# FFN of an adaLN transformer block: the last four token tiles as one group of 512 in place of two pairs, with a new order of issue on all engines

## The chip, the core and the metric

The kernel runs on one core of one Trainium2 chip. The metric is the device time of one execution in microseconds (us), lower is better; a time is the median of several executions. A core has a tensor engine (PE, matmuls), a vector engine (DVE), a scalar engine (ACT), a small general engine (POOL) and a sync engine (SP). Each has a queue of its own that it works through in order; an instruction that waits on a semaphore holds all that stand behind it in its queue. Here SP issues every DMA, plain copies and transposing ones alike.

## The reference

One transformer block with adaptive layer norm on x of 2048 tokens by 512 features, all in bfloat16. `c` is a conditioning vector.

```python
mod = (silu(c) @ w_mod).reshape(1, 6, 1, -1)
sa, ca, ga, sb, cb, gb = (mod[:, i] for i in range(6))
h = layernorm(x) * (1 + ca) + sa
x = x + ga * attention(h, wqkv, wo)
h = layernorm(x) * (1 + cb) + sb
x = x + gb * ((silu(h @ w1) * (h @ w3)) @ w2)
```

The attention has 32 heads of 16 features. Each token looks at 8 positions only: itself and those 2, 4, ... 14 tokens before it; positions before the start are masked out of the softmax. The FFN (w1, w3: 512 by 1792, w2: 1792 by 512) does most of the arithmetic.

## The kernel before

**Tiles and stages.** The tokens are 16 tiles of 128. The stages of a tile run through several engines: statistics of the first layer norm on DVE (`ln_stats`, L576; the normalised tile `xn` by L607), a transposition to features by tokens and the scaling with the modulation (`ln_T`, L644), the projections to q, k (`proj_qk`, L710, evicted by ACT L739 and L740) and v (`proj_v`, L744), local attention for pairs of tiles (products of q with shifted k on DVE L781, sums over features on PE L791, softmax with L808, L821, L833, L835, L836 and a transposition of the weights by PE L850; products of v with the weights on DVE L868 and L873, sums on PE L886, evicted to `ac` by ACT L892 and transposed to `ot` by DMA), the output projection (`project`, L895: PE L901, residual on DVE L906, with the sums that the second layer norm needs), the second layer norm (`ln_sums`, L613: ACT L617, L621, L627, POOL L629, ACT L633, L636), its transposition (`ln_T` again), and the FFN. `ffn_unit` (L911) computes one 128-wide piece of the hidden layer of a group of tiles: 4 matmuls with w1, ACT L924 for the silu, 4 matmuls with w3 (all by L918), DVE L933 for the product. There are 14 such units for each group. `ffn_w2` (L940) multiplies with w2 (PE L962; for the last two tiles in halves of 256 columns, L950), and `store` (L970) adds the residual on DVE L972 and sends the tile out.

**v goes through DRAM.** ACT evicts a tile's v from PSUM to one of three buffers, `v0` to `v2` (L760). SP stores it to `v_scratch_dram`, and shifted copies of it are loaded back as `vsh` (L858) for the attention. A buffer can be filled again only when the store of the tile before it has landed.

**wo** comes in four loads of 32 partitions' worth each and is scaled by ga in one DVE instruction (L987), which waits for all four. The output projection L901 waits for that.

**Groups.** `LN1` gives the groups of tiles for the first layer norm and the projections, `FFN` those for the second layer norm and the FFN. A matmul of a unit has as many columns as its group has tokens: 256 for a pair, 512 for four tiles. `DMA_T` says which groups are transposed by DMA (L652, issued by the common line L124, one DMA per tile, followed by four ACT instructions L656 on the whole group) and which by PE (L671, evicted and scaled by L679): the first tuple is for the groups of `LN1`, the second for those of `FFN`.

**The order of the work.** A class `Program` first records every operation with its engine, the values that it reads and writes, and their buffer pools. `ORDER` is a list of the numbers of the operations; `place` (L143) puts each at the end of its engine's queue in that order, and gives the values the buffers in `SLOTS` (eight PSUM banks, three `h`, four `q`, five `xn`, three `v` and others). `synchronize` (L165) works out which semaphores each must wait for, from data and from reuse of buffers, and `emit` (L208) writes the queues. So the two lists decide what stands behind what on every engine.

Of the kernel before, what the change touches and what calls it, by code (L numbers as in the profile page):

```python
# [264 lines left out]
FFN = [[0,1],[2,3],[4,5,6,7],[8,9,10,11],[12,13],[14,15]]  # L265
# [6 lines left out]
DMA_T = ((3, 4), (2, 3, 4, 5))  # L272
# [3 lines left out]
def _build(p, A_x, A_wqkv, A_wo, B_w1, B_w3, B_w2, c, w_mod, out):  # L276
# [364 lines left out]
    def pairs(Ts):  # L641
        return [Ts[i:i + 2] for i in range(0, len(Ts), 2)]

    def ln_T(which, gi, vns):  # L644
        vh = Val("h", hpool)
        vh.pieces = [Val(f"h_{ft}") for ft in range(KT)] if not which and not gi else None
        n = len(vns)
        if gi in DMA_T[which]:
            k = ("tr", 2 * gi + (2 * len(LN1) if which else 0))
# [365 lines left out]
    zold = []  # L1015
    for gi, Ts in enumerate(FFN):
        vns = [v for pr in pairs(Ts) for v in ln_sums(pr)]
# [116 lines left out]
```

## Time and profile before

| | |
|---|---|
| median of 3 runs | 238.24 us (237.93 to 238.61) |
| the profiled execution's own time | 237.94 us |
| its span in the profile | 236.2 us, clock of PE 0.999 of full |
| PE busy | 229.8 us, 97% of the span, 1768 matmul instructions |
| DVE, ACT, POOL busy | 178.8, 147.7 and 20.0 us |
| DMA | 40.42 MB, mean 171 GB/s |

The profile shows one execution. Its span runs from the first to the last recorded instruction; 1.7 us of the execution lie outside it. The page gives the busy time of each engine, the busy share in 40 slices of 5.9 us, and the chain of work that ended last. The timeline gives rows of one engine: start, duration, line, operation, output and input, count, and in brackets the idle time ahead of it and what ended that. SPq is SP's queue: a row there is the time that SP took to issue a DMA, not the time until its data landed; the latter is a line of its own, "DMA to landing". PE can run a weight load beside a matmul. Some matmul records are missing from the trace, so a row's count may be one or two short.

### The profile page before, as it was taken

To read this page: it belongs to the slowest core of one execution; us is meant where nothing else is said; L and a number is where in the kernel's file an instruction comes from. 1 tells how busy PE (TensorE), PEld (TensorE's weight loads), DVE (VectorE), ACT (ScalarE), POOL (GpSimd) and SP (SyncE) were. 2 spreads that over 40 slices of the span, in tenths; PEclk is the share of its full clock that TensorE was granted. 3 is DMA by queue.
4 is the path that set the end of the run, shared out by engine and by line. 5 is a ranking of instruction groups with operands and counts; after the bars stand their busy time and mean duration, and the time that the engine had idled before them with its cause. 6 is when DMAs were issued, how large, how long until landed. Compare 5 with 4: busy or idle time off the path is not lost.

```text
span 236.2 us, 4478 instructions
## 1 busy us (share of the span) xinstructions
PE 229.8 (97%) x1768; PEld 136.0 (58%) x1794; DVE 178.8 (76%) x286; ACT 147.7 (63%) x298; POOL 20.0 (8%) x44
## 2 busy tenths in 40 slices
PE   7999999999999999999999999999999999999995
PEld 5766554544597586564444444444465457485774
DVE  5598999999979999999999999793364403434433
ACT  3299587979989855985746786829866415040300
POOL 5432050002000000110001010001010000000000
PEclk9999999999999999999999999999999999999999
DMA  6999589999999783896591854441311000000202
GB/s 198 391 324 311 140 305 236 220 261 369 359 264 405 280 263 100 255 263 217 147 293 54 305 139 69 86 180 44 76 38 44 25 0 1 0 25 0 71 0 89
DMA packets 42717, 40.42 MB, mean 171 GB/s; under 512 B 23224, under 2 KB 39624, under 8 KB 40648
## 3 DMA queue, kind: packets, MB, share of 16 engines
q1 hardware_dynamic: 42688, 40.14, 57.4%
q8 instruction: 14, 0.23, 0.4%
q14 instruction: 7, 0.06, 0.1%
q10 hardware_dynamic: 8, 0.00, 0.0%
HBM read 30.67 MB, written 4.21 MB: 148 GB/s over the span
## 4 chain that ended last, share of the span: by engine, by line
PE 87%; DMA 4%; ACT 4%; DVE 1%; issue 1%; SPq 1%; POOL 0%; ACTq 0%
PE pall L918 41%; PE pall L962 18%; PE pall L728 7%; PE pall L901 5%; PE pall L750 4%; PE pall L886 3%; PE pall L791 3%; PE pall L950 3%; DMA sb_wm_s<-in_w_mod_dram 2%; DMA v_scratch_dram<-sb_v 2%; PE pall L671 1%; SPq L124 1%; ACT sb_xn L636 1%; ACT sb_xn L621 1%; ACT sb_q L739 1%
## 5 line engine op out<-in xcount | busy, mean ns | idle before, releaser
L918 PE MATMUL pall<-sb_h,sb_w 128*128 128x256 bf16 (+1 forms) x664 | 101.1, 307 | 0.6 <-ACT sb_ac L892 0.2
L918 PEld LDWEIGHTS pall<-sb_h,sb_w 128*128 128x128 bf16 x672 | 65.0, 98 | 35.8 <-issue 1.1
L933 DVE TENSOR_TENSOR sb_hh<-sb_sg,pall 128x256 bf16<-128x256 bf16 (+1 forms) x84 | 39.9, 506 | 36.7 <-PE pall L918 31.2
L924 ACT ACTIVATE sb_sg<-pall 128x256 bf16<-128x256 f32 (+1 forms) x84 | 36.0, 452 | 45.3 <-PE pall L918 41.9
L962 PE MATMUL pall<-sb_w,sb_hh 128*128 128x512 bf16 x190 | 44.0, 379 | 0.3
L781 DVE TENSOR_TENSOR sb_pq<-sb_q,sb_kT 128x4096 bf16<-128x4096 bf16 x16 | 36.4, 2285 | 0.0
L962 PEld LDWEIGHTS pall<-sb_w,sb_hh 128*128 128x128 bf16 x196 | 18.9, 98 | 21.7 <-issue 0.4
L728 PE MATMUL pall<-sb_h,sb_wqkv 128*128 128x512 bf16 (+1 forms) x156 | 30.3, 335 | 0.7 <-issue 0.4
L728 PEld LDWEIGHTS pall<-sb_h,sb_wqkv 128*128 128x128 bf16 x160 | 14.7, 98 | 11.9 <-ACT sb_v L760 0.8
L972 DVE TENSOR_TENSOR sb_o<-pall,sb_x 128x512 bf16<-128x512 f32 (+1 forms) x18 | 11.1, 628 | 9.7 <-PE pall L962 6.0
L629 POOL TENSOR_TENSOR sb_rs<-sb_rs,sb_cst 128x2 f32<-128x2 f32 x8 | 6.8, 855 | 135.4 <-ACT sb_rs L627 135.4
L656 ACT ACTIVATE sb_h<-sb_h,sb_modc 128x512 bf16<-128x512 bf16 (+1 forms) x24 | 16.3, 733 | 3.0 <-DMA sb_h<-sb_xn 3.0
L868 DVE TENSOR_TENSOR sb_vsh<-sb_vsh,sb_al 128x4096 bf16<-128x4096 bf16 x7 | 15.9, 2287 | 0.0
L750 PE MATMUL pall<-sb_wqkv,sb_h 128*128 128x512 bf16 x60 | 15.2, 379 | 0.3 <-issue 0.2
L901 PE MATMUL pall<-sb_wo,sb_ot 128*128 128x512 bf16 x60 | 14.7, 379 | 0.3 <-issue 0.2
L873 DVE TENSOR_TENSOR sb_vsh<-sb_vsh,sb_al 128x2048 bf16<-128x2048 bf16 x12 | 14.3, 1222 | 0.3 <-DMA sb_vsh<-v_scratch_dram 0.2
L892 ACT ACTIVATE sb_ac<-pall 128x512 bf16<-128x512 f32 x16 | 9.6, 604 | 5.7 <-PE pall L886 5.6
L679 ACT ACTIVATE sb_h<-pall,sb_modc 128x256 bf16<-128x256 bf16 (+1 forms) x18 | 9.8, 614 | 4.7 <-DVE sb_modc L536 3.8
L636 ACT ACTIVATE sb_xn<-sb_x,sb_nb,sb_rs 128x512 bf16<-128x512 bf16 x16 | 12.6, 807 | 0.1
L906 DVE SCALAR_TENSOR_TENSOR sb_x<-pall,sb_x 128x512 bf16<-128x512 f32 x16 | 10.9, 687 | 1.6 <-PE pall L901 1.5
L621 ACT ACTIVATE sb_xn<-sb_x,sb_nm 128x512 bf16<-128x512 bf16 x16 | 11.4, 715 | 0.2
L740 ACT ACTIVATE sb_kT<-pall 128x512 bf16<-128x512 f32 x16 | 9.4, 604 | 3.1 <-PE pall L728 3.1
(94 smaller groups left out, 212.7 us busy)
## 6 DMA issues: line engine op xcount, KB each, us to landing
sb_vsh<-v_scratch_dram SPq DMA_DIRECT2D x13, 1024.0 KB, 7.2
sb_w<-in_B_w_dram SPq DMA_DIRECT2D x6, 512.0 KB, 6.6
sb_vshx<-v_scratch_dram SPq DMA_DIRECT2D x3, 1024.0 KB, 6.5
sb_w<-in_B_w_dram SPq DMA_DIRECT2D x6, 384.0 KB, 6.3
sb_x<-in_A_x_dram SPq DMA_DIRECT2D x8, 256.0 KB, 6.9
v_scratch_dram<-sb_v SPq DMA_DIRECT2D x16, 128.0 KB, 6.2
out_dram<-sb_o SPq DMA_DIRECT2D x14, 128.0 KB, 2.3
sb_wqkv<-in_A_wqkv_dram SPq DMA_DIRECT2D x6, 256.0 KB, 6.3
```

Source lines behind the costliest of these rows:

```text
L636: p.op("act", lambda e, vn=vn, T=T: e.activation(vn.at[:], x_sb[:, T, :], ACT.Identity, bias=nb[:, T, :], scale=rs[:, NT + T, :]), c_act(5 ...
L656: return e.activation(vh.at[:, ft, 0:n * P], vh.at[:, ft, 0:n * P], ACT.Identity, bias=modc[:, 8 * which + ft:8 * which + ft + 1], scale=m ...
L728: ins = e.matmul(bank(vp)[:, j * n:(j + 1) * n], wqkv[:, t, col:col + P], vh.at[:, t, 0:n], start=(t == ORDER[0] and j == 0), stop=(t == O ...
L750: ins = e.matmul(bank(vp), vh.at[:, t, tt * P:(tt + 1) * P], wqkv[:, t, 2 * D:3 * D], start=(t == ORDER[0]), stop=(t == ORDER[-1]))
L781: return e.tensor_tensor(vp.at[:], in0, in1, ALU.mult)
L868: return e.tensor_tensor(v_w, v_w, a_w, ALU.mult)
L873: return e.tensor_tensor(v_w, v_w, a_w, ALU.mult)
L901: ins = e.matmul(bank(vy), bass.AP(vt.at, ft * 2 * P + a, [[KT * 2 * P, P], [step_, P]]), wo[:, ft, :], start=(ft == 0), stop=(ft == KT - 1))
L918: ins = e.matmul(bank(vp)[:, 0:n], wt[:, t, fi * P:(fi + 1) * P], vh.at[:, t, 0:n], start=(t == 0), stop=(t == KT - 1))
L924: p.op("act", lambda e: e.activation(vt.at[:, 0:n], bank(vgp)[:, 0:n], ACT.Silu), c_act(n), k, r=[vgp], w=[vt], table="silu")
L933: p.op("dve", lambda e: e.tensor_tensor(vh_.at[:, 0:n], vt.at[:, 0:n], bank(vup)[:, 0:n], ALU.mult), c_dve(n), k, r=[vt, vup], w=[vh_])
L962: ins = e.matmul(bank(vz), vhh[fi].at[:, tt * P:(tt + 1) * P], w2[:, fi, :], start=(fi == 0), stop=(fi == NF - 1))
```

## The change

Three things are edited. The last two FFN groups become one; the tuple of FFN groups that are transposed by DMA loses its last number, since there is one group fewer (the last group is transposed by DMA before and after); and `ORDER` and `SLOTS` are replaced as a whole. With the merge 1094 operations become 1034: 28 units of 256 columns become 14 of 512, and one layer norm's scaling, four ACT instructions L656, goes too.

```diff
-FFN = [[0,1],[2,3],[4,5,6,7],[8,9,10,11],[12,13],[14,15]]
+FFN = [[0,1],[2,3],[4,5,6,7],[8,9,10,11],[12,13,14,15]]
...
-DMA_T = ((3, 4), (2, 3, 4, 5))
+DMA_T = ((3,4),(2,3,4))
...
 ORDER = [
-    21, 20, 8, 0, 9, 18, 66, 22, 10, 11, 3, 67, 12, 4, 1, 68, 13, 23, 19, 69, 2, 70, 16, 24, 17, 71, 5, 72, 6, 62, 75,
+    21, 20, 8, 0, 9, 18, 66, 22, 10, 11, 3, 67, 12, 4, 1, 68, 13, 23, 19, 69, 2, 70, 16, 17, 24, 71, 5, 72, 6, 62, 75,
...
```

What the new lists do to the queues is shown at three places. The first is SP's queue in the opening, around the transposes of the last group of `LN1` (tiles 12 to 15, `h1`). `v0`, `v1`, `v2` are the buffers of v, `ot` the attention's output, `xn` the normalised tiles. Before:

```order
L124 DMA v_scratch_dram<-sb_v1 128x512
L124 DMA v_scratch_dram<-sb_v0 128x512
L124 DMA sb_wo<-in_A_wo_dram 32x4x512
L124 DMA_TRANSPOSE sb_h1<-sb_xn2 128x4x128
L124 DMA_TRANSPOSE sb_h1<-sb_xn4 128x4x128
L124 DMA_TRANSPOSE sb_h1<-sb_xn3 128x4x128
L124 DMA_TRANSPOSE sb_h1<-sb_xn0 128x4x128
L124 DMA sb_wo<-in_A_wo_dram 32x4x512 x2
L124 DMA sb_x<-in_A_x_dram 128x2x512
L124 DMA v_scratch_dram<-sb_v2 128x512
L124 DMA_TRANSPOSE sb_ot0<-sb_ac0 128x4x128
```

And now:

```order
L124 DMA v_scratch_dram<-sb_v1 128x512
L124 DMA_TRANSPOSE sb_h1<-sb_xn2 128x4x128
L124 DMA_TRANSPOSE sb_h1<-sb_xn1 128x4x128
L124 DMA_TRANSPOSE sb_h1<-sb_xn0 128x4x128
L124 DMA_TRANSPOSE sb_h1<-sb_xn3 128x4x128
L124 DMA v_scratch_dram<-sb_v0 128x512
L124 DMA sb_wo<-in_A_wo_dram 32x4x512
L124 DMA sb_x<-in_A_x_dram 128x2x512
L124 DMA sb_wo<-in_A_wo_dram 32x4x512 x2
L124 DMA v_scratch_dram<-sb_v2 128x512
L124 DMA_TRANSPOSE sb_ot0<-sb_ac0 128x4x128
```

The store from `v0` (v tile 4) and one load of wo stood ahead of the four transposes and now stand behind them; the next load of x moved ahead of two loads of wo. What follows on SP (the second transpose of `ot`, a load of w3, the next store from `v0`, which is v tile 10) is the same in both. Further on in the opening, one load of x that stood behind the loads of `vsh` is now issued earlier, and the load of a half of w_mod for the second modulation stands behind the transposes of the group before in place of ahead of them.

The second place is PE's queue from the last output projection (L901, tiles 14 and 15) on. `h2` is the input of the FFN group of tiles 8 to 11, `h0` before that of tiles 12 and 13, after that of 12 to 15. Before:

```order
L901 MATMUL pall<-sb_wo,sb_ot0 128x512 x8
L918 MATMUL pall<-sb_h2,sb_w3 128x512 x8
L918 MATMUL pall<-sb_h0,sb_w1 128x256 x8
L918 MATMUL pall<-sb_h0,sb_w3 128x256 x4
L918 MATMUL pall<-sb_h2,sb_w1 128x512 x4
L918 MATMUL pall<-sb_h0,sb_w1 128x256 x4
L918 MATMUL pall<-sb_h0,sb_w3 128x256 x4
L918 MATMUL pall<-sb_h0,sb_w1 128x256 x8
L918 MATMUL pall<-sb_h0,sb_w3 128x256 x4
L918 MATMUL pall<-sb_h0,sb_w1 128x256 x4
L918 MATMUL pall<-sb_h0,sb_w3 128x256 x4
```

And now:

```order
L901 MATMUL pall<-sb_wo,sb_ot0 128x512 x8
L918 MATMUL pall<-sb_h2,sb_w1 128x512 x4
L918 MATMUL pall<-sb_h2,sb_w3 128x512 x12
L918 MATMUL pall<-sb_h2,sb_w1 128x512 x4
L918 MATMUL pall<-sb_h2,sb_w3 128x512 x4
L918 MATMUL pall<-sb_h2,sb_w1 128x512 x4
L918 MATMUL pall<-sb_h2,sb_w3 128x512 x12
L918 MATMUL pall<-sb_h2,sb_w1 128x512 x4
L918 MATMUL pall<-sb_h2,sb_w3 128x512 x12
L918 MATMUL pall<-sb_h2,sb_w1 128x512 x4
L918 MATMUL pall<-sb_h2,sb_w3 128x512 x4
L918 MATMUL pall<-sb_h0,sb_w1 128x512 x4
```

Before, the matmuls of the pair 12 and 13 (256 columns) were mixed with those of tiles 8 to 11, and the pair 14 and 15 came later. Now 64 matmuls of tiles 8 to 11 follow the output projection, and the merged group, with 512 columns, begins behind them.

The third is ACT's queue at the same place, from the second layer norm of tiles 14 and 15 on (behind its L617). Before:

```order
L621 ACTIVATE sb_xn4,sb_var<-sb_x,sb_nm 128x512
L621 ACTIVATE sb_xn0,sb_var<-sb_x,sb_nm 128x512
L627 ACTIVATE sb_rs<-sb_var,sb_cst 128x2
L924 ACTIVATE sb_sg5_74<-pall 128x256
L924 ACTIVATE sb_sg4_73<-pall 128x512
L924 ACTIVATE sb_sg3_72<-pall 128x256
L633 ACTIVATE sb_nb<-sb_nm,sb_rs 128x1 x2
L924 ACTIVATE sb_sg2_71<-pall 128x256
L924 ACTIVATE sb_sg1_70<-pall 128x512
L636 ACTIVATE sb_xn4<-sb_x,sb_nb,sb_rs 128x512
L924 ACTIVATE sb_sg3_72<-pall 128x256
L636 ACTIVATE sb_xn0<-sb_x,sb_nb,sb_rs 128x512
```

And now:

```order
L924 ACTIVATE sb_sg5_74<-pall 128x512
L621 ACTIVATE sb_xn1,sb_var<-sb_x,sb_nm 128x512
L621 ACTIVATE sb_xn3,sb_var<-sb_x,sb_nm 128x512
L627 ACTIVATE sb_rs<-sb_var,sb_cst 128x2
L924 ACTIVATE sb_sg4_73<-pall 128x512
L633 ACTIVATE sb_nb<-sb_nm,sb_rs 128x1 x2
L636 ACTIVATE sb_xn3<-sb_x,sb_nb,sb_rs 128x512
L924 ACTIVATE sb_sg2_71<-pall 128x512
L636 ACTIVATE sb_xn1<-sb_x,sb_nb,sb_rs 128x512
L924 ACTIVATE sb_sg5_74<-pall 128x512
L924 ACTIVATE sb_sg0_69<-pall 128x512
L656 ACTIVATE sb_h0<-sb_h0,sb_modc 128x512 x4
```

Between L627 and the second L636 there stood six evictions L924 of units, of both widths; now there are two, of 512 columns each.

123 rows, old and new, of tables (ORDER, SLOTS) are left out of this document.

## The prediction, made before the run

> **What bounds the kernel now.** First the page: what share TensorE (PE) is busy, and where it is not.
>
> ```profile
> span 236.2 us, 4478 instructions
> PE 229.8 (97%) x1768; PEld 136.0 (58%) x1794; DVE 178.8 (76%) x286; ACT 147.7 (63%) x298; POOL 20.0 (8%) x44
> PE   7999999999999999999999999999999999999995
> ```
>
> PE is busy 229.8 of 236.2 us. Idle time lies in the first and the last slice, and little in between. So a change gains only by cheaper matmuls or by removing one of the few PE waits, and loses by any new wait. Next the windows view, to see which stretch still has PE waits, with columns in the order PE, weight loads, DVE, ACT, POOL:
>
> ```profile
> 40.00:60.00 20.00, 19.21 (x162) 9.37 (x163) 19.98 (x22) 18.23 (x38) 1.61 (x1) 1.00 1.05 268
> 180.00:200.00 20.00, 19.89 (x120) 11.72 (x120) 6.80 (x13) 7.99 (x18) 0.00 (x0) 1.00 0.09 20
> ```
>
> At 180 to 200 us, in the FFN, PE idles 0.11 us of 20, and DVE and ACT have most of their time free. At 40 to 60 us PE idles 0.79 us while DVE (19.98) and ACT (18.23) are nearly full: there a delay on any queue has little to be absorbed in. The chain of waits says who holds PE there:
>
> ```profile
> 46.51 0.58 SPq L124
> 47.09 0.05 issue
> 47.14 4.26 DMA v_scratch_dram<-sb_v
> 51.42 0.60 ACT sb_v L760
> 52.02 0.10 ACT sb_nm L617
> 52.15 1.52 ACT sb_xn L621 x4
> ...
> 57.16 1.53 ACT sb_xn L636 x2
> 58.69 0.05 issue
> 58.74 0.51 PE pall L671 x6
> ```
>
> Read backwards: the PE transposes L671 at 58.74 wait for ACT's L636, ACT works without a gap from 51.42, and at 51.42 it was released by a store of a v tile that SP issued at 47.14. That store could not start earlier because SP was issuing the work queued ahead of it. After 60 us the chain is PE with pieces of 0.05 us of "issue" and never leaves PE for long. Whatever moves SP's issue at 47.14 therefore moves the end.
>
> **The merge.** Groups [12,13] and [14,15] each run 14 units of 8 matmuls of 256 columns, 224 in all; one group of four tiles runs 112 of 512 columns. Rows of the chain for a run of each:
>
> ```profile
> 136.02 6.04 PE pall L918 x28
> 206.52 6.11 PE pall L918 x56
> ```
>
> 512 wide: 6.04/28 = 215.7 ns; two of 256: 2 × 6.11/56 = 218.2 ns. 112 × 2.5 ns = **0.28 us saved**. The gate and up evictions on ACT and DVE also halve in number, but PE never waits for them at 180 to 200 us, so that is worth nothing. [...]
>
> **The start of the last group.** Its LN2 can begin only when the residual of tiles 14 and 15 exists. Now tiles 12 and 13 wait for it too, so PE must be fed meanwhile; the new order puts 64 matmuls of group [8..11] there.
>
> ```profile
> 169.49 1.73 PE pall L901 x8
> 171.98 0.20 ACT L617 ACTIVATE sb_nm<-sb_sx 128x2 f32<-128x2 f32 x1 [1.55 <-DVE sb_x L906]
> 178.62 0.82 ACT L636 ACTIVATE sb_xn<-sb_x,sb_nb,sb_rs 128x512 bf16<-128x512 bf16 x1
> 179.47 2.52 SPq L124 DMA_TRANSPOSE sb_h<-sb_xn  x2
> DMA to landing us min/median/max: 2.3/2.4/2.4
> 31.02 2.92 ACT L656 ACTIVATE sb_h<-sb_h,sb_modc 128x512 bf16<-128x512 bf16 x4
> ```
>
> L901 ends at 171.22; 64 × 0.2157 = 13.8 us later, at 185.0, PE wants h. The chain for h: the second L636 ends at 179.44; of its two transposes the second is issued at about 180.7 and lands 2.4 us later, 183.1, and the first scaling L656 (2.92/4 = 0.73 us) ends at 183.9. Slack 1.1 us for the first matmul, which needs only that quarter of h; the other quarters follow every 0.73 us against 0.22 us of a matmul, so the fourth (186.1) meets a matmul due near 185.7: up to 0.4 us of wait if nothing comes sooner. In the new order two gate evictions stand between L627 and the second L636 in place of six, so I expect that chain a little sooner, and cost this part at nothing; its price without that cover is in a rival.
>
> **SP's queue in the opening.** This is the term that decides. Before, SP issued:
>
> ```profile
> 31.96 1.12 SPq L124 DMA_DIRECT2D v_scratch_dram<-sb_v  x2
> 33.12 0.60 SPq L124 DMA_DIRECT2D sb_wo<-in_A_wo_dram  x1
> 33.77 7.56 SPq L124 DMA_TRANSPOSE sb_h<-sb_xn  x4
> 41.37 1.23 SPq L124 DMA_DIRECT2D sb_wo<-in_A_wo_dram  x2
> 42.65 0.60 SPq L124 DMA_DIRECT2D sb_x<-in_A_x_dram  x1
> 43.29 0.60 SPq L124 DMA_DIRECT2D v_scratch_dram<-sb_v  x1
> 43.94 2.53 SPq L124 DMA_TRANSPOSE sb_ot<-sb_ac  x2
> ```
>
> The second store of the first row (v tile 4, buffer v0) and the wo load at 33.12 now stand behind the four transposes. If those could start as much earlier, SP would lose nothing. They can't, because their input isn't there:
>
> ```profile
> 32.60 0.41 DVE L607 TENSOR_SCALAR sb_xn<-sb_x,sb_mv,sb_rs 128x512 bf16<-128x512 bf16 x1
> 42.46 0.64 ACT L760 ACTIVATE sb_v<-pall 128x512 bf16<-128x512 f32 x1
> 42.94 0.65 ACT L892 ACTIVATE sb_ac<-pall 128x512 bf16<-128x512 f32 x1
> 45.92 1.22 DVE L987 TENSOR_TENSOR sb_wo<-sb_wo,sb_ga_bc 128x2048 bf16<-128x2048 bf16 x1
> 47.14 0.60 ACT L760 ACTIVATE sb_v<-pall 128x512 bf16<-128x512 f32 x1 [0.17 <-DMA v_scratch_dram<-sb_v]
> ```
>
> The first normalised tile is ready at 33.01, so the transposes start at 33.05 at best; a DVE that is later by half a microsecond, since four matmuls of v now stand ahead of work it waits for, gives about 34.1. I take 33.6: they end at 33.6 + 7.56 = 41.15. Step by step from there:
>
> 1. The store of v tile 4 is issued at 41.2 in place of 32.6. The store issued at 43.29 released ACT at 47.14, 3.85 us later; so this one lands at 45.0.
> 2. ACT's eviction of v tile 10 into the same buffer, at 42.46 before, must wait for it: 45.0, with the whole ACT queue behind it. The eviction L892 next to it starts 0.48 us later and takes 0.65: the second `ac` is ready at 46.13 in place of 43.6.
> 3. SP: 41.2 + five issues of 0.64 (store, wo, x, two of wo) = 44.4, the store of v tile 6 until 45.04, first transpose of `ot` until 46.3, the second (input ready) until 47.57, w3 0.63: the store of v tile 10 is issued at 48.2, against 47.14. That is **+1.06 us** on the store that the chain runs through. (A store that lands in 3.6 us and a start at 33.05 give +0.55; a landing of 4.26 as in the chain and a start at 34.1 give +1.8.)
> 4. ACT is back in time for it: the 1.27 us that it idled ahead of 51.42 take up the delay of step 2, so the delays are not added.
> 5. The last wo load is issued at 43.8 and lands about 3.85 later at 47.6, while DVE wants to scale wo (L987) at 45.92: DVE, full in this stretch, is 1.7 us later. Its results that PE needs next are these:
>
> ```profile
> 52.58 0.69 DVE L836 TENSOR_TENSOR sb_attn<-pall,sb_ssum 128x512 bf16<-128x512 f32 x1
> 57.59 2.28 DVE L868 TENSOR_TENSOR sb_vsh<-sb_vsh,sb_al 128x4096 bf16<-128x4096 bf16 x1
> 54.68 0.39 PE L850 MATMUL pall<-sb_ident,sb_attn 128*128 128x128 bf16 x4
> 61.52 0.60 PE L886 MATMUL pall<-sb_vsh,sb_ind 128*32 128x512 bf16 x8
> ```
>
> The softmax result is there at 53.27 and wanted at 54.68, the vsh product at 59.87 and wanted at 61.52: 1.4 and 1.65 us to spare, plus the 1.06 by which PE is late itself. Nothing more is lost.
>
> **Sum.** −0.28 + 1.06 = +0.78 us. Against the profiled execution (237.94 us: its span of 236.2 and 1.7 around it): 238.72. That execution is 0.3 us below the median of the three runs (238.24), so in terms of the median **239.0 us**. What the measurement can tell from no change is 0.3%, 0.71 us: faster is below 237.53, slower above 238.95.
>
> **Rivals.**
>
> *The transposes don't hold SP.* [...] If the four take 0.64 us each to issue, as the plain loads at 41.37, they end near 36.2, the store of v tile 4 lands near 40.1, ahead of 42.46, and no wait is new. Then only the merge is left: 237.96, no change that can be told. Against it stands the row of 7.56 us for four, 1.9 us each, under the load that will be there again; for it, the two later ones at 179.47, 1.26 us each with idle DMA engines.
>
> *Faster: the wait goes altogether.* The new order also takes one load of x out of the stretch from 42 to 51 us. If the store of v tile 10 is issued no later than 47.14 and lands in 3.6 rather than 4.26 us, ACT's chain moves up by 0.66 us, and at most the 0.79 us of PE idle time at 40 to 60 us go too: 238.24 − 0.28 − 0.79 = 237.2; half of it gives 237.5. It decides if SP gets the five issues behind the transposes out before 43.3, which needs transposes under 1.6 us each.
>
> *The last group starts late.* If its last two transposes land as slowly as those of the opening (4.7 us, the smallest that the answer for the stretch shows, in place of 2.4), h is late by 2.3 − 1.1 = 1.2 us for the first matmul, on top: 240.2. Decides where the chain behind L901 takes over 13.8 us. Against: the share of busy DMA in the windows rows, the last figure but one, is 0.09 at 180 to 200 us and 1.05 at 40 to 60.
>
> ```profile
> L124 SPq DMA_TRANSPOSE sb_h<-sb_xn x4: 1430/1878/2244, 33.8 to 39.2; - x4
> DMA to landing us min/median/max: 4.7/7.4/8.7
> ```
>
> **How the numbers follow.** Forecast 0.53, of which 0.10 (the low end of the delay, +0.27 net, 238.5) falls within 0.3%; transposes that don't hold SP 0.23; the wait gone 0.16; last group late 0.07; the cheap wide matmul 0.01. So faster 0.17, same 0.33, slower 0.50. The forecast's own range is 238.5 to 239.8 (+0.55 and +1.8, less 0.28). The range over all: low 237.5, which takes in the second case and the slower half of the third; high 239.9.
>
> **What would show it.** Right: in the changed profile SP's four transposes of h start near 33.6 and end near 41; ACT's L760 around 42.5 carries a wait of some 2 us for the v store; the store behind w3 is issued near 48.2; PE's L671 and L728 near 59 are a microsecond late; the L918 of the last group have 216 ns each and no wait ahead of them. Wrong: no ACT wait at 42.5, or that store issued at 47.1 or sooner (first or second rival); a PE wait near 185 us for h (third); a wait in the FFN that is in none of these.

## The result and the profile after

The changed kernel takes 240.55 us (median of 22 runs, 238.28 to 241.78), the kernel before 238.78 (22 runs, 237.23 to 240.92): a ratio of 1.0061, 95% interval 1.0037 to 1.0084, or about 1.5 us; the two medians are 1.77 us apart. The ratios here and below leave out executions more than 1.5% above the fastest of their kernel (three of twelve for m3, a kernel below). The sign is the forecast's, and the waits that it described are in the trace. The time lies above the range, at twice the loss forecast: PE also waited where the sum had nothing, and the kernel before itself turned out slower than its first three runs said.

The profiled execution after took 239.92 us, with a span of 238.2. The page and the windows view show the same picture as before, a little looser:

```profile
span 238.2 us, 4250 instructions
PE 231.4 (97%) x1682; PEld 124.7 (52%) x1682; DVE 177.6 (75%) x272; ACT 144.9 (61%) x280; POOL 20.1 (8%) x44
```

```profile
20.00:40.00 20.00, 19.39 (x192) 10.62 (x190) 19.20 (x29) 15.56 (x28) 4.20 (x7) 1.00 1.12 262
40.00:60.00 20.00, 18.55 (x154) 8.51 (x153) 18.44 (x22) 16.03 (x33) 1.71 (x1) 1.00 0.93 247
180.00:200.00 20.00, 20.00 (x94) 9.07 (x93) 9.11 (x14) 9.77 (x17) 0.00 (x0) 1.00 0.09 20
```

PE idles 1.45 us between 40 and 60 us where it idled 0.79, and not at all between 180 and 200. In these FFN windows it has 94 matmuls and no wait.

The useful way to compare two such traces is by marks: instructions that every version has, and the time from one to the next. I use the first matmul L531 (near 7.5 us), the first L791 of the second attention block (27 us), the first output projection L901 (48 us), the first transpose L671 behind it (58 us), the next L791 (61 us) and the end. Rows of three of them before, with that of L514, of which more below, from the timeline of PE:

```profile
27.09 0.29 PE L791 MATMUL pall<-sb_before,sb_ones 128*32 128x256 bf16 x4
31.93 0.94 PE L514 MATMUL pall<-sb_csT_bf,sb_wm_s 128*128 128x1 bf16 x32
48.19 1.89 PE L901 MATMUL pall<-sb_wo,sb_ot 128*128 128x512 bf16 x8
58.35 0.89 PE L671 MATMUL pall<-sb_ident,sb_xn 128*128 128x128 bf16 x8
```

and after, with what PE waited for in brackets:

```profile
21.97 0.54 PE L558 MATMUL pall<-sb_csT_bf,sb_wm_g 128*128 128x1 bf16 x16 [0.61 <-DMA sb_wm_g<-in_w_mod_dram]
27.86 0.29 PE L791 MATMUL pall<-sb_before,sb_ones 128*32 128x256 bf16 x4
34.42 0.94 PE L514 MATMUL pall<-sb_csT_bf,sb_wm_s 128*128 128x1 bf16 x32
50.19 1.89 PE L901 MATMUL pall<-sb_wo,sb_ot 128*128 128x512 bf16 x8 [1.07 <-DVE sb_mx L803]
60.59 0.91 PE L671 MATMUL pall<-sb_ident,sb_xn 128*128 128x128 bf16 x8
```

PE is 0.77 us late at the first mark, 2.00 at L901, 2.24 at L671, and 1.98 at the end (the last L972 starts at 235.74 in place of 233.76): the FFN gives 0.25 back. So the loss stands in three places: ahead of 27 us, between there and L901, and a little more up to L671, the only place where the prediction had a term. The wait of 0.61 ahead of L558 has two causes. This second group of the gate's products now stands earlier in PE's queue (it ran at 25.73 us before), and two loads of x are now issued right behind the gate's load, which lands in 11.6 us in place of 9.9.

Between 34 and 51 us the predicted waits are seen. SP, ACT and DVE there, from the timeline after:

```profile
34.39 7.85 SPq L124 DMA_TRANSPOSE sb_h<-sb_xn  x4
42.29 0.58 SPq L124 DMA_DIRECT2D v_scratch_dram<-sb_v  x1
...
44.96 0.60 ACT L760 ACTIVATE sb_v<-pall 128x512 bf16<-128x512 f32 x1 [1.18 <-DMA v_scratch_dram<-sb_v]
...
46.14 2.62 SPq L124 DMA_TRANSPOSE sb_ot<-sb_ac  x2
48.21 1.23 DVE L987 TENSOR_TENSOR sb_wo<-sb_wo,sb_ga_bc 128x2048 bf16<-128x2048 bf16 x1 [1.20 <-DMA sb_wo<-in_A_wo_dram]
49.44 0.57 SPq L124 DMA_DIRECT2D v_scratch_dram<-sb_v  x1
```

The four transposes hold SP for 7.85 us; the store behind them goes out at 42.29, ACT waits 1.18 us for it, DVE waits 1.20 for wo, and the store of v tile 10 goes out at 49.44, 2.30 us later than before, where 1.06 was forecast. The row of L901 names DVE's L803, on which L901 doesn't depend. What it waits for is the scaling of wo (L987, done at 49.44) and the two transposes of `ot`; the second of these was issued near 47.5 and landed some 2.5 us later, near 50, so it came last.

The chain of waits after runs through that store as it did before, and then through an FFN stretch of 112 wide matmuls in a row:

```profile
47.73 1.04 SPq L124
48.76 0.04 issue
48.81 0.58 SPq L124
49.39 0.05 issue
49.44 4.07 DMA v_scratch_dram<-sb_v
...
59.41 1.53 ACT sb_xn L636 x2
60.94 0.05 issue
60.99 0.51 PE pall L671 x6
...
173.47 24.17 PE pall L918 x112
```

24.17 / 112 = 215.8 ns each, and no wait where the last group begins.

### The profile page after: what moved, and what is told of

It reads as the page before. It is cut to its first block, busy times and chain, and to the rows that moved or that the text cites. A ratio compares the mean times of both kernels' runs of the same rounds, so it can differ in the third digit from the quotient of the medians.

```text
span 238.2 us, 4250 instructions
## 1 busy us (share of the span) xinstructions
PE 231.4 (97%) x1682; PEld 124.7 (52%) x1682; DVE 177.6 (75%) x272; ACT 144.9 (61%) x280; POOL 20.1 (8%) x44
## 4 chain that ended last, share of the span: by engine, by line
PE 83%; DMA 7%; SPq 4%; ACT 4%; issue 1%; DVE 0%
PE pall L918 41%; PE pall L962 18%; PE pall L728 6%; PE pall L901 5%; DMA sb_wm_g<-in_w_mod_dram 5%; SPq L124 4%; PE pall L886 3%; PE pall L791 3%; PE pall L750 3%; PE pall L950 3%; DMA v_scratch_dram<-sb_v 2%; ACT sb_q L739 1%; ACT sb_xn L636 1%; ACT sb_xn L621 1%; ACT sb_kT L740 1%
## 5 line engine op out<-in xcount | busy, mean ns | idle before, releaser
L918 PE MATMUL pall<-sb_h,sb_w 128*128 128x512 bf16 (+1 forms) x560 | 101.3, 337 | 0.0
L918 PEld LDWEIGHTS pall<-sb_h,sb_w 128*128 128x128 bf16 x560 | 54.2, 98 | 45.4 <-issue 0.8
L933 DVE TENSOR_TENSOR sb_hh<-sb_sg,pall 128x512 bf16<-128x512 bf16 (+1 forms) x70 | 38.1, 574 | 34.5 <-PE pall L918 30.6
L924 ACT ACTIVATE sb_sg<-pall 128x512 bf16<-128x512 f32 (+1 forms) x70 | 34.0, 508 | 37.3 <-PE pall L918 34.7
L962 PE MATMUL pall<-sb_w,sb_hh 128*128 128x512 bf16 x196 | 44.6, 379 | 0.0
L781 DVE TENSOR_TENSOR sb_pq<-sb_q,sb_kT 128x4096 bf16<-128x4096 bf16 x16 | 36.3, 2282 | 0.3 <-ACT sb_q L739 0.3
L728 PE MATMUL pall<-sb_h,sb_wqkv 128*128 128x512 bf16 (+1 forms) x160 | 31.0, 337 | 0.4 <-ACT sb_v L760 0.4
L972 DVE TENSOR_TENSOR sb_o<-pall,sb_x 128x512 bf16<-128x512 f32 (+1 forms) x18 | 11.3, 628 | 13.1 <-PE pall L962 8.9
L728 PEld LDWEIGHTS pall<-sb_h,sb_wqkv 128*128 128x128 bf16 x160 | 14.7, 98 | 12.0 <-ACT sb_v L760 1.3
L656 ACT ACTIVATE sb_h<-sb_h,sb_modc 128x512 bf16<-128x512 bf16 x20 | 15.0, 808 | 4.7 <-DMA sb_h<-sb_xn 4.7
L901 PE MATMUL pall<-sb_wo,sb_ot 128*128 128x512 bf16 x64 | 15.6, 379 | 1.1 <-DVE sb_mx L803 1.1
L750 PE MATMUL pall<-sb_wqkv,sb_h 128*128 128x512 bf16 x64 | 16.1, 380 | 0.0
L636 ACT ACTIVATE sb_xn<-sb_x,sb_nb,sb_rs 128x512 bf16<-128x512 bf16 x16 | 12.6, 807 | 0.1
L760 ACT ACTIVATE sb_v<-pall 128x512 bf16<-128x512 f32 x16 | 9.7, 603 | 2.8 <-DMA v_scratch_dram<-sb_v 2.5
```

Source lines behind the costliest of these rows:

```text
L636: p.op("act", lambda e, vn=vn, T=T: e.activation(vn.at[:], x_sb[:, T, :], ACT.Identity, bias=nb[:, T, :], scale=rs[:, NT + T, :]), c_act(5 ...
L656: return e.activation(vh.at[:, ft, 0:n * P], vh.at[:, ft, 0:n * P], ACT.Identity, bias=modc[:, 8 * which + ft:8 * which + ft + 1], scale=m ...
L728: ins = e.matmul(bank(vp)[:, j * n:(j + 1) * n], wqkv[:, t, col:col + P], vh.at[:, t, 0:n], start=(t == ORDER[0] and j == 0), stop=(t == O ...
L750: ins = e.matmul(bank(vp), vh.at[:, t, tt * P:(tt + 1) * P], wqkv[:, t, 2 * D:3 * D], start=(t == ORDER[0]), stop=(t == ORDER[-1]))
L781: return e.tensor_tensor(vp.at[:], in0, in1, ALU.mult)
L901: ins = e.matmul(bank(vy), bass.AP(vt.at, ft * 2 * P + a, [[KT * 2 * P, P], [step_, P]]), wo[:, ft, :], start=(ft == 0), stop=(ft == KT - 1))
```

## The experiments

The edit of most kernels is a move of operations in the list `ORDER`, which sets each engine's order. The helper is this:

```diff
+def moved(order, ops, ahead):
+    rest = [o for o in order if o not in ops]
+    i = rest.index(ahead)
+    return rest[:i] + ops + rest[i:]
```

Operation 227 is the store of v tile 4, 43 the load of wo that was moved with it, 349 the second group of matrix-vector products for the gate (L558), 36 to 40 loads of x, 47 and 48 the two half loads of w_mod for the second modulation, 46 a small store of zeros (`zrow`). None of the kernels leaves out work. Ratios are to the kernel before on the same chip. The steps are those between the marks above, from one profiled execution of each.

| kernel | ratio [95% interval] | 7.5→27 us | 27→48 | 48→58 | 61→end |
|---|---|---|---|---|---|
| before | 1 | 19.56 | 21.10 | 10.16 | 175.15 |
| after | 1.0061 [1.0037, 1.0084] | 20.29 | 22.33 | 10.40 | 174.90 |
| *early loads as after* | | | | | |
| e1 gate group back | 1.0052 [1.0017, 1.0087] | 20.01 | 21.56 | 10.17 | 174.88 |
| e2 two SP issues back | 1.0028 [0.9993, 1.0063] | 19.66 | 21.98 | 10.35 | 174.94 |
| e3 both | 1.0057 [1.0023, 1.0091] | 20.01 | 21.85 | 10.32 | 174.89 |
| h2 opening of after, no merge | 1.0089 [1.0051, 1.0128] | 19.72 | 22.57 | 10.34 | 175.14 |
| f3 opening of before, SP of after | 1.0047 [1.0012, 1.0082] | 19.56 | 22.27 | 9.72 | 175.68 |
| j2 after, order behind 30 us old | 1.0057 [1.0027, 1.0088] | 19.89 | 22.85 | 10.15 | 174.96 |
| k2 as j2, two SP issues back | 1.0069 [1.0038, 1.0099] | 19.70 | 21.64 | 10.17 | 175.52 |
| m3 opening of before, early loads of after | 1.0077 [1.0040, 1.0113] | 19.56 | 24.95 | 9.72 | 174.93 |
| *early loads as before* | | | | | |
| e4 before, two SP issues late | 1.0049 [1.0012, 1.0086] | 19.55 | 23.54 | 9.86 | 175.39 |
| e9 before, the store late | 1.0015 [0.9987, 1.0042] | | | | |
| e10 before, the wo load late | 1.0008 [0.9975, 1.0041] | 19.56 | 21.87 | 9.74 | 175.75 |
| f1 after with SP of before | 1.0039 [1.0008, 1.0070] | 19.62 | 22.80 | 10.28 | 174.90 |
| g1 before, DVE 0.95 us later | 0.9996 [0.9962, 1.0030] | 19.56 | 22.06 | 9.78 | 175.22 |
| h1 merge alone | 0.9998 [0.9967, 1.0030] | 19.56 | 21.62 | 9.93 | 174.84 |
| i1 as h1, v10's store ahead of w3 | 1.0002 [0.9967, 1.0038] | | | | |
| j1 as h1, ACT's order of after | 1.0009 [0.9982, 1.0036] | 19.57 | 22.13 | 10.35 | 175.20 |
| m1 as h1, PE and DVE of after ahead of 35 us | 0.9990 [0.9964, 1.0015] | 19.62 | 21.96 | 10.08 | 175.58 |
| m2 as m1, gate group back | 1.0016 [0.9991, 1.0040] | 20.02 | 21.91 | 10.17 | 174.94 |

The traces of e9 and i1 began with a PE wait of 1.51 us (at most 1.02 us at that place in the others), and their steps are left out. Single executions of one kernel differ by up to 3.7 us (the 22 of the kernel before), so the ratios decide, and the steps only show where a given execution lost its time.

**The theories.** The prediction's: the two issues moved behind the transposes cost about 1.06 us and the merge gives 0.28. Its rivals, formed from the trace: the order of PE, DVE and ACT ahead of 30 us costs (the gate's wait, DVE 0.4 us later); or SP's other loads ahead of 30 us do.

**1. Undo one part of the changed kernel (e1, e2, e3).**

```diff
+ORDER = moved(ORDER, [349], 215)        # e1, e3
+ORDER = moved(ORDER, [227, 43], 308)    # e2, e3
```

> The changed kernel with one operation moved back: the 16 matmuls L558 of the second gate stand behind the fifth projection again, where they stood before, and not directly behind the 16 of the first gate. Theory A (the loss has two places that add up: a wait of PE for the load of w_mod's gate columns at 22 us, 0.6 to 0.8 us, and SP's queue around the four transposes, 1.0 to 1.5 us; the merge gives 0.28 back): PE's wait of 0.61 us at 21.97 goes, the work at 28 us is 0.6 to 0.8 us earlier, and the time is that of the changed kernel less 0.7, about 0.7 us above before. Rival B (the first wait is covered by what comes later, so that only the second place counts): no change against the changed kernel, 1.4 us above before.

> The changed kernel with two DMA issues moved back: the store of v tile 4 and one load of wo stand ahead of the four transposes of h again. Theory A: ACT's wait of 1.2 us at 44.96, DVE's 1.2 us ahead of L987 and PE's 1.07 us ahead of L901 go; the second place is worth 1.0 to 1.5 us, so the time is 0.3 to 0.6 us above before (the gate's wait, 0.77, stays, the merge gives 0.28 back). Rival B: with the second place undone the first one shows in full or is covered by the slack at 60 us; then the time is that of before or 0.3 us below it. Rival C (the order of these issues doesn't matter, the loss is spread over the new order): 1.4 us above before.

> The changed kernel with both moved back: the gate's matmuls and the two DMA issues. What is left of the change is the merge and the rest of the new order. Theory A: 0.28 us below before, and in the profile PE reaches the transposes L671 near 60 us within 0.3 us of before. Rival C (the loss is spread over the new order): still 0.5 us or more above before.

None comes back to 1. The gate's wait of 0.61 us is gone in e1, but PE meets another right behind, in the matmuls that now come first (timeline of e1):

```profile
21.34 2.76 PE L728 MATMUL pall<-sb_h,sb_wqkv 128*128 128x512 bf16 x12 [0.31 <-ACT sb_h L679]
```

With the two issues back (e2), ACT's wait for the v store goes, but wo is still late, since a load of x stands ahead of its last two loads and the transposes took 8.34 us there:

```profile
33.99 8.34 SPq L124 DMA_TRANSPOSE sb_h<-sb_xn  x4
...
47.35 1.22 DVE L987 TENSOR_TENSOR sb_wo<-sb_wo,sb_ga_bc 128x2048 bf16<-128x2048 bf16 x1 [0.75 <-DMA sb_wo<-in_A_wo_dram]
```

e2 is 0.33% quicker than the changed kernel, but its interval holds 1.0061 too, and e3, with the same two issues back, shows no gain.

**2. The suspected cost alone, on the kernel before (e4, e9, e10).**

```diff
+ORDER = moved(ORDER, [227, 43], 42)     # e4; e9: [227], e10: [43]
```

> The kernel before with one thing of the change: the store of v tile 4 and one load of wo stand behind the four transposes of h. Theory A, by the sum of the prediction: 1.06 us above before (0.55 to 1.8), with ACT's eviction of v tile 10 waiting some 2 us for that store at 42.5 and DVE's L987 waiting for wo. If the transposes then start at 33.05 in place of 33.77, since nothing stands ahead of them, 0.55 to 0.9. Rival C (SP's order doesn't matter): no change.

> The kernel before with only the store of v tile 4 behind the four transposes of h (the load of wo stays ahead). Theory of the prediction (ACT waits for that store, the second transpose of ot and the store of v tile 10 come later): ACT waits 1 to 2.5 us at about 42.5 to 45, and the time is 0.5 to 1.1 us above before. Rival (it is wo that costs, through DVE): within 0.3 us of before.

> The kernel before with only the one load of wo behind the four transposes of h. By step 5 of the prediction: DVE waits about 1 us ahead of L987 at 46 us and nothing more is lost, within 0.3 us of before. Theory A3 (DVE is full from 22 to 60 us, so every wait of DVE there comes out at the end): 0.5 to 1.0 us above before.

Both issues late cost 0.49%, 1.17 us of 238.63 (0.3 to 2.1 by the interval): the size forecast. The trace of e4 shows the chain as predicted, and one step more, PE itself waiting at L901 for the attention's output:

```profile
43.63 0.60 ACT L760 ACTIVATE sb_v<-pall 128x512 bf16<-128x512 f32 x1 [1.40 <-DMA v_scratch_dram<-sb_v]
48.45 1.23 DVE L987 TENSOR_TENSOR sb_wo<-sb_wo,sb_ga_bc 128x2048 bf16<-128x2048 bf16 x1 [0.86 <-DMA sb_wo<-in_A_wo_dram]
50.86 1.89 PE L901 MATMUL pall<-sb_wo,sb_ot 128*128 128x512 bf16 x8 [1.35 <-DMA sb_ot<-sb_ac]
```

Either issue alone costs 0.15% or 0.08%, not told from nothing.

**3. The merge alone, and the opening alone (h1, h2).** h1 takes the order of the first 500 operations from the kernel before and the rest from the changed one; h2 the reverse, with the groups unmerged. `SLOTS` is fitted to each.

> The merge alone: the first 500 operations (to about 75 us, all engines) in the order of before, the rest in the order of the changed kernel, with the last four tiles as one group. Theory A (all that is lost is lost in the opening; the merge gives 0.28 us): 0.28 us below before, with the stretch from the L791 at 61 us to the end 0.25 shorter than before's 175.15. Rival (the new order loses in its tail as well, where no trace shows a wait): at or above before.

> The opening alone: the first 500 operations in the order of the changed kernel, the rest as before, in two pairs. Theory A: the whole loss of the changed kernel and the 0.28 us that the merge gave: 1.5 to 2 us above before. Rival: half of it or less.

The merge alone is worth nothing that can be measured in the time; in the trace its last step is 174.84 against 175.15. Nine traces of merged kernels lie at 174.84 to 174.96 there, and those of unmerged ones at 175.14 to 175.75; four merged ones (f3, j1, k2, m1) took 175.20 to 175.68, three of them with one PE wait of 0.42 to 0.64 us. The loss is in the opening: h2, which has the new opening alone, shows all of it.

**4. SP's queue, exchanged as a whole (f1, f3).**

```diff
+# f1, on the changed kernel
+ORDER = moved(ORDER, [46, 47], 36)
+ORDER = moved(ORDER, [36], 177)
+ORDER = moved(ORDER, [40], 150)
+ORDER = moved(ORDER, [39], 369)
+ORDER = moved(ORDER, [227, 43], 308)
+ORDER = moved(ORDER, [37], 233)
+ORDER = moved(ORDER, [38], 288)
```

f3 is the counterpart: h1, with these loads and the two issues where the changed kernel has them.

> The changed kernel with SP's queue in the opening as before (all loads, stores and transposes in the old order); PE, ACT, DVE and POOL as changed. Theory A2 (SP's order costs 1.2 to 1.5 us, the other engines' order 0.45 by the step from 7.5 to 27 us, the merge gives 0.28): 0.2 us above before. Rival B2 (the other engines' order costs it, SP's issues only show it): 1.2 us above before.

> The merge with the opening of before, but SP's queue in the opening in the order of the changed kernel; PE, ACT, DVE and POOL as before. Theory A2: 1.2 to 1.5 less 0.28, so about 1.0 us above before, with waits for the store of v tile 4 and for wo between 42 and 50 us. Rival B2: 0.28 us below before.

SP's new queue alone costs 0.47% (f3), and with SP's old queue 0.39% are left (f1), so each looks like the cause and the sum of the parts is larger than the whole. In f3's trace PE waits for the later of the two half loads of w_mod, issued at 29.41 where the kernel before issues its later one at 18.50:

```profile
33.40 0.95 PE L514 MATMUL pall<-sb_csT_bf,sb_wm_s 128*128 128x1 bf16 x32 [1.01 <-DMA sb_wm_s<-in_w_mod_dram]
```

**5. Other engines (g1, i1, j1, j2, k2).** g1 adds to the kernel before a DVE product of 0.95 us, which nothing reads, ahead of the first L781 (its lines stand one further down); i1 puts v10's store ahead of w3's load; j1 gives h1 the order of ACT's two evictions L740 and L739 near 50 us; j2 is the changed kernel with the order of operations from about 30 to 75 us as before, except SP's, which puts back ACT's evictions, one DVE instruction and some buffers; k2 is j2 with the two issues, and a load of x, back.

```diff
+ORDER = moved(ORDER, [285], 53)                                         # i1
+ORDER = moved(moved(ORDER, [322], 570), [314], 328)                     # j1
+ORDER = moved(moved(ORDER, [227, 43], 308), [37], 233)                  # k2
```

> The kernel before with one more DVE instruction, a product of 128x1536 ones into a buffer that nothing reads, of about 0.95 us, ahead of the first L781 at 22.2 us. Theory A3 (DVE is full from 22 to 60 us and PE follows it): 0.7 to 0.95 us above before, and L901 and L671 later by as much. Rival (PE's queue and the DMA set these times, and DVE has slack to PE): within 0.3 us of before.

> The merge with the opening of before, and the store of v tile 10 ahead of the load of w3 on SP. If that store releases ACT and so PE at 59 us, as the chain of before shows: issued 0.6 us sooner, ACT's wait at 51.4 and PE's at 52.1 and 59.4 us get smaller, and the time is 0.3 to 0.5 us below the merge alone, 0.5 to 0.8 below before. Rival (DVE's queue sets PE's times there): the same as the merge alone, 0 to 0.3 us below before.

> The merge with the opening of before, and one thing of the changed order: on ACT, an eviction of k (L740) ahead of L617 in place of behind L627, and an eviction of q (L739) behind L627, at about 52 us. In the traces so far the step from the first L901 to the L671 near 59 us is 9.7 to 10.2 us in the kernels with the old order there (mean 9.92) and 10.2 to 10.4 in those with the new one (mean 10.31). Theory C (ACT's order there costs that 0.4 us): step 10.3, time 0.4 us above the merge alone, 0.1 to 0.3 above before. Rival (the step is longer because SP or DVE is late, not by ACT's order): step 9.9, time as the merge alone.

> The changed kernel with ACT's and DVE's order from about 50 us to 75 us as before (L740 behind L627, one L833 sooner); everything ahead of 50 us, SP and PE as changed. Theory C: step from L901 to L671 9.9 us in place of 10.3, time 0.4 us below the changed kernel, about 0.9 above before. Rival: step 10.3, 1.2 to 1.4 us above before.

> The kernel of the run before this one with SP's issues around the four transposes as before too: the store of v tile 4 and the load of wo ahead of them, the load of x behind the other two loads of wo. What is left of the new order is what lies ahead of 30 us: PE's and DVE's order around the layer norm of tiles 4 to 7, the second gate's matmuls, loads of x and of w_mod. Theory: 0.3 us for that (step from 7.5 to 27 us 19.6 to 20.3 in place of 19.56), less 0.28 for the merge: at before, within 0.3 us. Rival (what is left ahead of 30 us makes everything later on worse): 0.7 us or more above before.

An extra 0.95 us on DVE at 22 us costs nothing that can be measured, though DVE is still 0.6 us late at its scaling of wo and PE then waits 0.41 us at its L901: my theory of the late DVE falls, if narrowly, since g1's interval reaches +0.7 us, where that theory begins. ACT's order and i1's store do nothing that can be told on h1 either. j2, with ACT's order put back, keeps the loss, and so does k2, with the two issues put back as well: what is left in k2 is the order of PE and DVE ahead of 35 us, SP's loads and v stores there, and some buffers.

**6. These two, apart (m1, m2, m3).** m1 has the whole SP queue of the kernel before and k2's order on the other engines; m3 has k2's SP queue and the other engines of h1; m2 is m1 with the gate group back.

```diff
+# m1: j2 with the seven moves of f1; m2: and
+ORDER = moved(ORDER, [349], 215)
+# m3, on h1
+ORDER = moved(ORDER, [36, 38], 46)
+ORDER = moved(ORDER, [39], 48)
+ORDER = moved(ORDER, [46], 48)
+ORDER = moved(ORDER, [40], 253)
+ORDER = moved(ORDER, [47], 369)
```

> Merged group; SP's queue as in the kernel before; ahead of 30 us only TensorE and VectorE stand as in the changed kernel (one statistics instruction between the normalised tiles, tile order of the transposes, four k matmuls and the second gate group early); behind that everything as before. If the order of these engines is what costs: 1.004 to 1.007, about 239.9 us. If it is the early loads on SP, or if both are needed together: 0.999 to 1.001, about 238.8.

> The same, with the second gate group back behind the first matmuls of the third v group. If the cost is a gate that waits for its load: 0.999 to 1.001. If it is VectorE's statistics instruction, 0.4 us later from 17 us on, with the tile order: as the kernel with the gate early, 1.004 to 1.007. If it is SP: 0.999 to 1.001 in both.

> Merged group; all of TensorE, VectorE and ScalarE as in the kernel before; SP ahead of 34 us as in the changed kernel (x loads early, the half load of w_mod late), the v store and the wo load ahead of the four transposes as before. If the early loads cost: 1.004 to 1.007, with a TensorE wait of about 1 us for the late half load near 33 us. If it is the order of the other engines, or both are needed: 0.999 to 1.001.

k2 and m1 have the same order and buffers on PE, DVE and ACT and differ on SP alone. From its queue's order, with − as in m1 and + as in k2 (`wm_g` is the gate's load, `wm_s` a half load of w_mod):

```
 L124 DMA sb_wm_g_82<-in_w_mod_dram 128x4x512
+L124 DMA sb_x<-in_A_x_dram 128x2x512 x2
+L124 DMA v_scratch_dram<-sb_v 128x512 x2
+L124 DMA sb_x<-in_A_x_dram 128x2x512
 L124 DMA v_scratch_dram<-sb_zrow 16x512
-L124 DMA sb_wm_s_76<-in_w_mod_dram 128x4x512
-L124 DMA v_scratch_dram<-sb_v 128x512
-L124 DMA sb_x<-in_A_x_dram 128x2x512
-L124 DMA v_scratch_dram<-sb_v 128x512
 L124 DMA sb_wm_s_76<-in_w_mod_dram 128x4x512
 L124 DMA_TRANSPOSE sb_h<-sb_xn 128x4x128
-L124 DMA sb_x<-in_A_x_dram 128x2x512
 L124 DMA v_scratch_dram<-sb_v 128x512
-L124 DMA_TRANSPOSE sb_h<-sb_xn 128x4x128 x3
-L124 DMA sb_x<-in_A_x_dram 128x2x512
+L124 DMA_TRANSPOSE sb_h<-sb_xn 128x4x128 x2
+L124 DMA sb_x<-in_A_x_dram 128x2x512
+L124 DMA_TRANSPOSE sb_h<-sb_xn 128x4x128
+L124 DMA sb_wm_s_76<-in_w_mod_dram 128x4x512
...
-L124 DMA sb_x<-in_A_x_dram 128x2x512
```

They measured 1.0069 [1.0038, 1.0099] against 0.9990 [0.9964, 1.0015]. The intervals do not touch. And m3 differs from h1 in the same moves on SP alone: 1.0077 against 0.9998, again 0.79%. So **SP's early order costs about 1.9 us on these two orders of the engines** (0.4 to 1.2% by the intervals of k2 and m1), and the order of PE and DVE ahead of 35 us costs nothing by itself (m1 against h1). The nine kernels of the table that have this order, the changed one among them, lie 0.28 to 0.89% above the kernel before, 0.60 in the mean. Of those with the early loads of before, all but two lie within −0.10 and +0.16: e4, whose cause is known, and f1.

A third pair doesn't agree. e2 and f1 both have the changed kernel's own order and buffers on PE, DVE and ACT, and the two issues ahead of the transposes; they differ in the same early moves on SP and in the place of one more load of x. e2, with the early order, is at 1.0028 [0.9993, 1.0063], f1, without it, at 1.0039 [1.0008, 1.0070]. By these intervals an early order that costs up to some 0.35% there is possible, one that costs 0.79% is not. So in the surroundings that the changed kernel has, the cost of the early order isn't shown.

How m3 loses is plain in its trace. PE waits 2.01 us for the late half load, and is then granted half its clock for some microseconds (timeline, and the windows view with the granted clock as the last figure but two):

```profile
33.76 0.95 PE L514 MATMUL pall<-sb_csT_bf,sb_wm_s 128*128 128x1 bf16 x32 [2.01 <-DMA sb_wm_s<-in_w_mod_dram]
34.58 1.02 PE L750 MATMUL pall<-sb_wqkv,sb_h 128*128 128x512 bf16 x4
35.44 3.33 PE L728 MATMUL pall<-sb_h,sb_wqkv 128*128 128x512 bf16 x8
```

```profile
36.00:37.00 1.00, 1.00 (x4) 0.45 (x3) 0.81 (x1) 0.00 (x0) 0.00 (x0) 0.50 1.07 295
37.00:38.00 1.00, 1.00 (x4) 0.31 (x3) 0.00 (x0) 0.91 (x2) 0.00 (x0) 0.50 0.72 242
38.00:39.00 1.00, 1.00 (x7) 0.59 (x6) 0.00 (x0) 0.38 (x2) 0.00 (x0) 0.50 1.05 361
```

Eight matmuls L728 take 3.33 us; the eight that follow L750 at the same place in h1 take 1.89. Seven of the nine executions of m3 that were compared had a mean clock of 0.993, and took 239.88 to 242.01 us; the two at 1.000 took 238.69 and 239.01. Where k2 loses isn't seen: its one trace is of the shortest of its twelve executions, 238.72 us, and has no such wait.

In the changed kernel it is not so plain, since there PE comes to L514 a group of eight matmuls (1.73 us) later. L514 reads both half loads, so the later one counts. The DMA answers for it, before and after:

```profile
L124 SPq DMA_DIRECT2D sb_wm_s<-in_w_mod_dram x1: 436/436/436, 18.5 to 18.5; - x1
DMA to landing us min/median/max: 5.7/5.7/5.7
```

```profile
L124 SPq DMA_DIRECT2D sb_wm_s<-in_w_mod_dram x1: 585/585/585, 29.4 to 29.4; - x1
DMA to landing us min/median/max: 4.0/4.0/4.0
```

Before, it lands at 24.2 and is wanted at 31.93: 7.7 us of slack. After, it lands at 33.4 and L514 starts at 34.42: 1.0 us of slack. (They aren't the same half: the one that goes out last after was issued at 13.33 us before.) The same load took 3.9 to 5.0 us to land in the other traces that have it there, and in h2 and j2 it landed 0.1 us ahead of its matmul. So a slower landing could stall PE in some executions of the changed kernel, but in the one that was traced it did not, and a halved clock is no large part of the loss: 19 of its 22 executions had a mean clock of 0.999 or 1.000, with a median of 240.35 us. The waits that its trace does show are the one for the gate, and those at 42 to 50 us.

**What stays open.** Which of the early moves (the half load, the pair of x loads behind the gate's load, or the stores between them) costs how much wasn't tried apart, and whether they cost the changed kernel anything is open by the third pair. Nor is f1 settled: it differs from m1 only in the order of ACT and DVE behind 30 us and in some buffers, and is 0.49% slower, with intervals that overlap between 1.0008 and 1.0015, while the same exchange on the changed kernel does nothing (j2, 1.0057 to 1.0061). In f1's trace the time goes in one wait that no theory here has, of DVE for a load of `vsh` and of PE behind it; in m1 PE waits 0.68 us at that L886, in the kernel before both waits are absent:

```profile
41.20 2.29 DVE L868 TENSOR_TENSOR sb_vsh<-sb_vsh,sb_al 128x4096 bf16<-128x4096 bf16 x1 [1.64 <-DMA sb_vsh<-v_scratch_dram]
43.63 0.62 PE L886 MATMUL pall<-sb_vsh,sb_ind 128*32 128x512 bf16 x8 [1.47 <-ACT sb_ac L892]
```

No version here is faster than the kernel before by what can be measured.

## Why the prediction was right and wrong

- **What bounds the kernel, and the merge.** Right: PE bounds it, and a wide matmul costs 215.8 ns (215.7 forecast). The step from 61 us to the end is 0.25 us shorter (0.28 forecast). In the time alone h1's interval of ±0.3% holds it as well as nothing.
- **The start of the last group.** Right: costed at nothing, and PE runs 112 matmuls there without a pause. The rival of a late last group falls. No run shows the cheap wide matmul that has 0.01 in the forecast's chances: those 112 took 24.17 us, 215.8 ns each.
- **SP's queue in the opening, steps 1 to 4.** The waits are as described, and the size agrees where nothing else is changed: e4 measured 1.17 us for 1.06, though the late store alone, on which steps 1 to 3 rest, cost 0.15% (e9), which isn't told from nothing. The transposes hold SP, 7.85 us for four after, 7.56 before, where plain issues on the same queue took 0.6 us each, so the rival in which they don't falls. In the changed kernel, though, undoing the two issues gains nothing that can be told: three kernels without them (e2, e3, k2) have a mean of 0.51%, the three with them (after, e1, j2) 0.57%. By these figures its delays aren't simply added to whatever else the new order costs.
- **Step 5, "Nothing more is lost".** Wrong. It followed DVE's products to the softmax and to vsh, not to PE's next instruction: PE waited 1.07 us at L901, for which wo must be scaled and `ot` transposed; both were late, and the transpose came last.
- **The wait goes altogether (faster).** Wrong: it counted the load of x that left the stretch from 42 to 51 us as relief for SP, and didn't ask what that load meets where it went.
- **The sum is the step that failed.** "−0.28 + 1.06" begins SP's account at 31.96 us and puts all that SP issues ahead of that at nothing, without a reason. Two loads of x now go out right behind the gate's load, and the later half load goes out 11 us later (29.44 for 18.50); the slack of the latter before (7.7 us) was not compared with the move. What the runs show in its place: PE is 0.77 us late at 27 us already, and 2.00 at L901. In the pairs m3 against h1 and k2 against m1 the early order costs 0.79%, 1.9 us; with the merge that would be −0.28 + 1.9 = 1.6 us, and 1.5 were measured, of 238.78, with an interval of 0.9 to 2.0. This agreement isn't proof: e2 and f1, with the changed kernel's own engines, show no such cost, so how much of the 1.5 us is the early order's, how much the two issues', stays open. That the order of the engines was costed at nothing, without an argument, holds for PE and DVE ahead of 35 us (m1) and for ACT's (j1, j2); f1 leaves it unsettled for the whole.
- **The reference point.** The three runs ahead of the prediction had a median of 238.24; 22 runs have 238.78. That shift alone is 0.5 us of the distance between 239.0 and 240.55. As a difference the range was +0.27 to +1.52 us, and the 1.5 us measured lie at its upper end. So a part of the miss is the reference's, and the missing terms are the rest.

## What to carry to other kernels

When a new order is costed, list every transfer that moved, with its landing and the start of its first reader before, and take the move from that slack: where the last load that a matmul needs goes out 11 us later and had 7.7 us of slack, that is a term of the sum even if PE never waited for it before. Then test by adding one part to the old kernel as well as by undoing one part of the new one: where two waits stand beside each other, undoing either may show nothing. And make the same exchange in more than one surrounding before calling it the cause: here it cost 0.79% in two and nothing that could be told in a third. Compare traces by steps between marks, but let repeated times decide, since one execution is only one draw.

## What the runs showed of the hardware

In these traces a PE wait could have a second price. Behind a wait of 2.01 us in a busy stream (m3) the granted clock fell to 0.50 for three windows of 1 us, with 0.86 and 0.93 in the windows on either side, so for about 3.4 us in all (0.28 + 3 + 0.14, an estimate from these figures that takes the clock for 1.00 or 0.50), and eight matmuls took 3.33 us in place of 1.89; behind one of 1.51 us at the start of e9 it fell as well, to 0.65, 0.50, 0.50 and 0.64 in the windows from 10 to 14 us. Behind 1.07 us (the changed kernel at L901), 1.35 (e4) and 1.47 (f1) the mean clock stayed at 1.00.

What is issued behind a load seems to change when it lands, though few traces say so: the slower of the gate's two loads took 9.9 us before, with a small store behind it, and 11.6 after, with two loads of x. Where the gate's second group stands early in PE's queue, it waited 0.61 us (after) and 0.19 (j2) for that load with the loads of x behind it, and in e2, h2 and k2 both groups took 1.04 to 1.10 us; with the small store there (f1, m1) they took 0.94, with no wait. And four transposes in a row held the queue for 6.32 (e1) to 8.94 us (m3) over the twenty traces; what sets it wasn't tried.
